# Scores on either kind of TensorE tiles, from exchanged copies of K and Q, in a windowed attention kernel

## The chip, the cores and the metric

The kernel runs on one core of one Trainium2 chip. The metric is device time in microseconds of one execution; of each kernel several runs are made and the median is taken. One profiled execution of the kernel before gives the views of the profile that are shown here.

Engines are named as the profile names them: PE (TensorE matmuls), PEld (its weight loads), DVE (VectorE), ACT (ScalarE), POOL (GpSimd) and SP (SyncE, which issues most of the DMAs; SPq is its queue).

## The reference

The input x is 224 × 224 pixels of 96 channels in bfloat16. One projection makes q, k and v. The first 48 channels attend within horizontal strips of 8 rows, the other 48 within vertical strips of 8 columns. A strip has 1,792 tokens and there are 28 of each kind. The two results stand side by side and go through a last projection.

```python
qkv = jnp.einsum('bhwc,cd->bhwd', x, wqkv)
...
scale = C2 ** (-0.5)
...
ah = _softmax(jnp.einsum('bqc,bkc->bqk', qh, kh) * scale, axis=-1)
oh = jnp.einsum('bqk,bkc->bqc', ah, vh).reshape(B, H, W, C2)
...
av = _softmax(jnp.einsum('bqc,bkc->bqk', qv, kv) * scale, axis=-1)
ov = jnp.einsum('bqk,bkc->bqc', av, vv).reshape(B, nw, H, sw, C2)
...
return jnp.einsum('bhwc,cd->bhwd', o, wo)
```

## The kernel before

**Blocks and halves.** Two strips make a block; there are 28 blocks (`P`), 14 horizontal and then 14 vertical. One strip lives on partitions 0 to 63 and the other on 64 to 127, of Q (`QT_sb`), K (`KT_sb`) and the values (`V_sb`). Every PE step of the main loop is a pair of matmuls, one for each strip (`w` is 0 or 1).

**Two kinds of tiles.** PE is used as four 64 × 64 tiles. A matmul whose operands lie on one half of the partitions can write to the same half or to the other half. When both strips write to their own half, the pair is on the *straight* tiles (mode "q"); when both write to the other half, it is on the *crossed* tiles (mode "v"). A step on straight tiles and a step on crossed tiles can run at the same time. Each kind has its own semaphore. Scores (`qk`, line 778) are on straight tiles and value products (`pv`, line 804) on crossed ones, except for the first four half key tiles (`turned`, `TURN = 2`), where it is the other way about. K, Q and most V projections (lines 535 and 637) are on straight tiles.

**A unit.** The queries of a block are cut in four chunks (512, 512, 512 and 256 columns). A unit is one chunk against 128 keys (256 for the short chunk): two score steps, called halves here, an exponential, and the products with V. There are 49 units in a block. Of 1,372 units 984 are ACT's: two halves fill two PSUM banks, one activation (line 824) reads both and writes one of eight `PT` buffers, two steps multiply by V. The other 388 are DVE's, taken in 194 pairs: DVE turns each half's scores into integers (line 844) in an `I_sb` buffer, two further operations (line 849, on POOL, or on DVE where the order says so) make `U_sb` and `E_sb` from it, and all three, read as bfloat16, are multiplied by V (`V_sb` twice, the scaled `Vs_sb` once). So a DVE unit has six value steps where an ACT unit has two. There are four buffers each of `I_sb` and `U_sb` (`NY`) and two of `E_sb` (`NL`). The first write of a pair into its `I_sb` waits for the products that read the pair `NY` back.

**The rest of a block.** `prep` projects K, Q and V of the next block from `xa_sb`/`xb_sb`, while the present one runs; DVE evicts them (lines 549, 556, 642). A chunk's sum is evicted to `OT_sb` (line 870) and projected by `wo` (lines 691, 725). Vertical blocks add the horizontal part from `Ph_sb` on POOL (line 733) and are stored by SP in 24 DMAs each (line 760). `blocks` (line 411) copies the input strips of a block into DRAM in block form, and `load` (line 418) transposes them into SBUF; both are on SP's queue.

**The order.** All operations are put in streams, one letter each. The string `SEQ` gives the order in which they are taken, and so the order on every engine; `BANK` gives the PSUM bank of each step that starts one. `Work.run` follows the strings and derives every wait from the operations' dependences, so an engine runs its list in order and waits where it must. The letters that the text uses: `a` a score half of an ACT unit, `A` its exponential, `c` its value step; `b` a score half of a DVE unit, `j` DVE's integer conversion, `U` or `u` the operations of line 849 on POOL or DVE, `d` and `D` the value steps with `I_sb`/`U_sb` and with `E_sb`; `e` evictions, `f` the projections, `h` the first of them; `X` and `x` loads and block transfers, `y` stores. `SEQ` and `BANK` were made ahead of time by a planner that isn't part of the kernel; the occupancies and latencies in the `Op` calls are its inputs and have no effect on the chip.

Of the kernel before, what the change touches and what calls it, by code (L numbers as in the profile page):

```python
# [23 lines left out]
def ndc(P, c):  # L24
# [9 lines left out]
    "fDjDAbcaceadfdAjdadaddecUdbAdadjafcDcAXXDebacajcbcUAcajcacbccAjcfaadodffAdbkeUadaddgjADbDacarjcbcAacrackcUjbdA"
    "fcacaejdfdAdabeadfdfUAXjcfabacecdAXcdadjabDdDAjbcacaDjfDAcaceUacDccAbaoaDcjbAgadardUjfdfAdfadradDfeADacaeccbVc"
    "fAajcaccbecAacjacUdbdAajdadbdjbddADaDajDdUDAacDcacbcDcAjdbacacjdUbAcajdadbdAodaDaDdjcdAcUdadagcbcArDcracacDcjA"
    "bcUacajgccAraodardbdgAdajUdadfDrAgarDacecfAcacreacUcbAdardadfdjdAbDaDeaDfDAdjacacdecdUAbdadjaDbDcAXXajcacbccAj"
    "bkcaUcacjcccAfadoadfdfAadaedkdbUcgAjcbDaDajcfcAacraecrbcfUcAjdadadebdAadadjdbdcdAXcjaUbaDdjDDAXabaffjDfAcDeacU"
    "accDAbcacjacccbcAoadaUdfjdAagadedffdfAracracDfDAebaUacecfcAcaedajdbdAadjbdadVdcjdAcbDaDjaDbDAdcUjacacbcdAcjaca"
    "cbcDAcjacUabDoAadadjdgddAdcrabraUcdDjdADbaDajDcbcAacjacfcUcAcaecagccAoadrardggUADaraDrddfrAdbrdacacjbcAUacacef"  # L40
    "cDAjDaDaDbecfAcaceacDdjbkdAadkajdDbdAjaUabdddddAXXjcacacbcAcjbacaUcccjcAfadaodfDfAbDaedadUgdjAdbacacrjcbcAaDra"
    "DDfjUDbAadadejdfdAadeaddcdcAXUbacajbdcdAXcDjabaDcjAcbUacacjcfcfAacaccfcbAoaaUcegAdadrajdfdAdraDaDfefdfAUabaecf"
    "ccjAbcacaecfcAcaVjcacbdedAadjbdadjbdAdUDaDajDdDbAcacjacbcdAcjaUcabdcDjbADcadajdAbdaodaUcdcdjcAdadagcbDrADDraca"
    "UcDcjbAcacajccgcAoaadrdbrUdgAdadrajDfDAdragacecfUAcacreaccfdAraddadbedfAdacajcbDADeaDajbkdDdkAcjdaUdaDbDcAXXaj"
    "cacbccAjbcacaUcjcccAfadoadfdfAadaedbdUDfAjDbcacaejcbcAacajcgdbUdArdajdadfrdAaDeaDdbdDAXUDjdabaccjdcAXfafafcbec"
    "DAacUacjcbcDAcajbacccjcAbadUaodfDAdjadadfdfefAaDageUcbcAracraccfjcAacacebcVcfAjadaddbedAadjbdaUDdDjdADbDacjacb"
    "cAdcjacaUcdbDAcajcabDoAdadadjUgdAdDarDarcdcbAcdajbadcDUcAjgaaccrDcrbAacacjccAUaodadbggAjdadadrdbArDaDarcjfUcAc"
    "acradfdedAadacebcfdAdjacacdDeAUbdaDajDbdADdjaDabcDjAXXcbcUacajcfcAcaecacbccAjafakcUofAdfdaaeddbAgdajdaDbDkrcAr"
    "aUcadjfdbdAcaecjadfcAcaceaUcfdfAXfadeabdDDdAXjafaDdbedADacaUjcDcbAcacjacbcDAcjabacccjcUAbaadodfDffAjadaddfedAa"
    "ceacVDbcfAjcacacbecAacUjadbddjbdAagadjdddDAaDrUaDrDbcdAjcaacbccdAcjabaUcDjcDAbacajdbddAjadacUcbocdAdaadjDgDdAc"  # L50
    "argarcDUcDArcarcacbcAccjcadaodbUAaDjaDcfcdgAbedadacrcjbAUdadadrfddAjgaadeddcAdcUarcarbdcAdDjabaDDjAfDaDaeUfcDc"
    "AXXaceacbccAjbacaccjkcccAfkadoaUdffAdaedadgdbArDfarDaccUejbAcacacjbcfdAdjadadbedAacacjbfdfAXcfjabUacDedDAXdadj"
    "abDdDAjDcacUacbcAcDjacaccccAbaoadUdfdjAdfadaedfDfAaDeagcfUcrAbracacedfAdadaeddjbAcVacajcbccAjbacaccjbDUAddaacj"
    "dcDbADaDjacbcdAcjdUcabaoDADajbadgddAjadUaDdrDdrcAbadajdcbcADcjacUagDcArcbrcacaccjAcaadoUdfdAadeadDgbDArdajcacf"
    "UcrAcbdaedadfdAjdadagebDADaDrajbDAcracUacdjcdAbdadjabcDcAXXDjcacaUcbcAacjacfcccecAfaodadbkdfUAgdjadadfrbDAraDa"
    "ceccAakjacUbddfjdbAdacaecjfdAdaceaUcdDdAXbaDajbdDdDAXDjabaDcUjcbAcacajccffAcfcaeacccUAcboaaddfjDAagaDedffAdfUr"
    "dardacfcAeabacecfdAcaVjcacbceAadjbdaddjbAddacacjUdDDAaDbaDcjbcdAacjacbcdcUAjabacDcjDbAadaodcAcjbUadadgjcdADdad"
    "rabrDdcADcjaUgacDrcAbrcacaccjcAaoadUdbdfAjdadadeDgbADacracjUbccAracagjcfdAdardeadfUdAcracaddecdAbacajDdbdDAjaf"
    "aDeDDDAXXbcaucaccAjbcakcakcjcccAfaodaUdfdfADbaeDaddgjAdbDaDarjUDbDAacracfcjcbAcacaejcfcAbadeaUdDdDAXdjabadddjd"
    "cAXdadabucfAcfacjacfcAbecacacjccAcbaoadUdfcAjaDaDbedfAfadjadfUdbAecaaccfjcAcbeacagcjVAdadadbrdfrdAadaDeUdDjdDA"  # L60
    "bcacjaDcbAcdjacacbUccdAjabaccDjDbAadaodDUAdjbadaDdcjdAcgadarbcrdcADUcacjacbcADcjagaccrcAoaUdardbdgAjdadadbrcfA"
    "rDDajcaUgcAaecacfcrDrAbcacadefdAdajdabdedAdUDaDajDdbAdadjabcDcDAXXjcaUcacbcfAcjacacccecAfaodakdbUDfADfjadadebd"
    "AdgaacrcrckcAUajadfdddbeAacajcbdfdAjcacaDdeDUdAXbdDajbaDDcAXDjabadcjcbUAcacjacffAcfcaeacccAbcUoadadfjdAbadaedf"
    "fAdfjaDgaDecbAUacrjaddbdAracacfcjcAacacVefdcbAecadajdbcdUAcjdcacaDbDAaDjbDacdcjdAbUacajcDbDAaodaddjbgAdaUDarDj"
    "dcdAcdardabcDcAjDgacUacrcbrAacacjccbAcoadajUdbAgdajgaddrdAbrDaDarcjfUcAcacracfcAedadadfedAdUadeabdcdcAjdbaDaDj"
# [12 lines left out]
    "DjbgAdadardfrdfAfdajdaDfDeAcaUcaecbcfAcjacacbecAacjacbcVcjbdAaaddjbddAdddaUjaDDbDdADjaabcDcjDAacabUcdcjbAcadaj"
    "dbddAoaDaDUdcjgcAdadrabrcdcADcjacacUbcADgjacaccrcAoaraddgbdUArdardadfDjADagaecfcAcUarceacbccAracadfjddAfdeadUa"
    "ddDeAdDabaDdjbdDAaDjaDkbcUcAXXjacacbccAjbcacacjcccAkfaUdoadfdfAdbaedadDgjADfacaUcercbrcfAcacjaccbAadeaddfqjfdf"  # L80
    "AabeaDfDUDAXjabaDdeddAXdcDjabaDcUjdAcacacbcdcAjfcacacfcbAUoaacjbfAdadaedgdjAdgVadacrcbrADaDarcjfcqcAarcaccfedb"
    "ADqaDajDbDAcjacUadbedAdjbacacdjbddAacacjUdccdAabacjbdcDADjadaUdboADaDadjbddcAdajdabcdcugAcacarcuDcDAcacraUcccj"
    "AgadardodbArdadadjgqDfAcracraDfcqecAacacedfdqAbddeaaccfUydjAbdacaeycDjAdbyaDaDjdbyADdkuadaDycDjcbAkacUyacjcbcA"
    "yacjaccfyocAbdayUjdadbAdfyajdadDfygDAfeacacyUcrcebArcyacadjfdyAdadeaDybDqfADfjaybaDjcfycAaUabedfydcAjdayadcdeb"
    "cAydcUajcacybcADcjacyacDbcoAyaUajbcygAdajdaXDgDrAdfradadUfrdfArcbacadeXdfAdjadacfcqebcAacaedddjXdcAqbDaDjaDbDA"
# [100 lines left out]
class Work:  # L186
# [29 lines left out]
    def run(s, seq, digits):  # L216
        at = {k: 0 for k in s.streams}
        digits = iter(digits)
        freed = {b: [] for b in range(8)}
        vlock = None  # L220
        for c in seq:
            both, q = c == "p", {"p": "P", "u": "U"}.get(c, c)
            op = s.streams[q][at[q]]
# [12 lines left out]
            if q != c:  # L236
                op.eng, op.fn = "dve", op.alt
# [697 lines left out]
```

## Time and profile before

| | us |
|---|---|
| median of 3 runs | 948.07 (947.41 to 948.56) |
| the profiled execution | 947.77 |
| its span, first to last instruction | 945.7 |
| busy: PE, ACT, DVE, POOL | 936.0, 925.2, 881.6, 769.2 |

The granted TensorE clock was 0.997 over the span. In a group of instructions the columns are line, engine, operation, output and inputs with their shapes, and the count; behind the bar the busy time in us, the mean duration of one in ns, and the idle time before them with what ended it. In a line of waits the numbers are total us, times, and the longest. In a line of the timeline they are start and duration in us. Records of one engine overlap, as an instruction starts while the one before drains, so a busy share close to 100% doesn't by itself say that an engine couldn't do more.

### The profile page before, as it was taken

To read this page: it belongs to the slowest core of one execution; us is meant where nothing else is said; L and a number is where in the kernel's file an instruction comes from. 1 tells how busy PE (TensorE), PEld (TensorE's weight loads), DVE (VectorE), ACT (ScalarE), POOL (GpSimd) and SP (SyncE) were. 2 spreads that over 40 slices of the span, in tenths; PEclk is the share of its full clock that TensorE was granted. 3 is DMA by queue.
4 is the path that set the end of the run, shared out by engine and by line. 5 is a ranking of instruction groups with operands and counts; after the bars stand their busy time and mean duration, and the time that the engine had idled before them with its cause. 6 is when DMAs were issued, how large, how long until landed. Compare 5 with 4: busy or idle time off the path is not lost.

```text
span 945.7 us, 48281 instructions
## 1 busy us (share of the span) xinstructions
PE 936.0 (99%) x21770; PEld 625.8 (66%) x21770; DVE 881.6 (93%) x1754; ACT 925.2 (98%) x993; POOL 769.2 (81%) x512
## 2 busy tenths in 40 slices
PE   9999999999999999999999999999999999999997
PEld 4666766676776677666666767766666666667664
DVE  8999999999999999999999999999999999999994
ACT  7999999999999999999999999999999999999996
POOL 3778988888886888787898888889879888878883
PEclk9999999999999999999999999999999999999998
DMA  8724513440441343244120515545533534461112
GB/s 141 96 46 72 71 22 53 71 66 9 71 71 22 52 72 47 28 71 71 28 46 10 93 36 81 88 72 86 86 61 67 85 57 81 76 84 30 31 20 44
DMA packets 253254, 57.09 MB, mean 60 GB/s; under 512 B 252936, under 2 KB 252936, under 8 KB 253048
## 3 DMA queue, kind: packets, MB, share of 16 engines
q1 hardware_dynamic: 251464, 53.47, 36.5%
q8 instruction: 170, 2.79, 1.3%
q10 hardware_dynamic: 1584, 0.55, 0.3%
q14 instruction: 36, 0.29, 0.1%
HBM read 19.13 MB, written 28.21 MB: 50 GB/s over the span
## 4 chain that ended last, share of the span: by engine, by line
PE 98%; ACT 1%; DVE 0%; issue 0%
PE ps L804 50%; PE ps L778 36%; PE ps L535 5%; PE ps L637 4%; PE ps L691 1%; PE ps L725 1%; ACT PT L824 1%; PE ps L396 0%; PE ps L602 0%; DVE out_sb L736 0%; PE ps L634 0%; PE ps L496 0%; PE ps L529 0%; DVE OT_sb L870 0%; DVE warm L368 0%
## 5 line engine op out<-in xcount | busy, mean ns | idle before, releaser
L824 ACT ACTIVATE PT<-ps 128x1024 bf16<-128x1024 f32 x984 | 921.2, 1036 | 7.7 <-PE ps L778 3.0
L778 PE MATMUL ps<-QT_sb,KT_sb 49*64 49x512 bf16 (+1 forms) x6272 | 738.8, 354 | 0.7 <-issue 0.6
L844 DVE TENSOR_SCALAR I_sb<-ps 128x512 int16<-128x512 f32 x776 | 511.1, 682 | 21.7 <-PE ps L778 17.2
L804 PE MATMUL ps<-PT,V_sb 64*50 64x512 bf16 (+1 forms) x4496 | 499.4, 350 | 0.2 <-issue 0.2
L778 PEld LDWEIGHTS ps<-QT_sb,KT_sb 49*64 49x64 bf16 x6272 | 282.3, 105 | 159.0 <-ACT PT L824 53.7
L849 POOL TENSOR_SCALAR U_sb<-I_sb 128x2048 int16<-128x2048 int16 x170 | 322.5, 1897 | 55.6 <-DVE I_sb L844 37.0
L849 POOL TENSOR_SCALAR E_sb<-I_sb 128x2048 int16<-128x2048 int16 x164 | 311.1, 1897 | 46.2 <-PE ps L804 18.9
L804 PE MATMUL ps<-U_sb,V_sb 64*50 64x512 bf16 (+1 forms) x1776 | 245.7, 350 | 0.0
L804 PE MATMUL ps<-I_sb,V_sb 64*50 64x512 bf16 (+1 forms) x1776 | 239.7, 352 | 0.2
L804 PEld LDWEIGHTS ps<-PT,V_sb 64*50 64x50 bf16 x4496 | 215.6, 100 | 32.7 <-issue 0.7
L804 PE MATMUL ps<-E_sb,Vs_sb 64*50 64x512 bf16 (+1 forms) x1776 | 233.2, 350 | 0.0
L733 POOL TENSOR_TENSOR out_sb<-tmp,Ph_sb 128x480 bf16<-128x480 f32 (+1 forms) x84 | 85.7, 1028 | 31.0 <-DVE E_sb L849 14.9
L804 PEld LDWEIGHTS ps<-I_sb,V_sb 64*50 64x50 bf16 x1776 | 80.2, 100 | 31.4 <-PE ps L804 8.2
L804 PEld LDWEIGHTS ps<-U_sb,V_sb 64*50 64x50 bf16 x1776 | 89.2, 100 | 14.0
L804 PEld LDWEIGHTS ps<-E_sb,Vs_sb 64*50 64x50 bf16 x1776 | 88.0, 100 | 13.8 <-issue 0.6
L535 PE MATMUL ps<-xa_sb,w_sb 64*64 64x512 bf16 (+3 forms) x440 | 80.2, 356 | 0.2 <-issue 0.2
L870 DVE CAST OT_sb<-ps 128x512 bf16<-128x512 f32 x112 | 68.9, 615 | 9.2 <-PE ps L804 8.5
L535 PE MATMUL ps<-xb_sb,w_sb 64*64 64x512 bf16 (+2 forms) x436 | 77.1, 348 | 0.0
L556 DVE TENSOR_SCALAR_CACHE_REDUCE KT_sb<-ps,bias 128x512 bf16<-128x512 f32 x108 | 72.0, 677 | 1.9 <-PE ps L535 1.5
L549 DVE TENSOR_SCALAR QT_sb<-ps 128x512 bf16<-128x512 f32 (+1 forms) x111 | 67.5, 615 | 3.2 <-PE ps L535 1.8
L637 PE MATMUL ps<-w_sb,xa_sb 64*64 64x48 bf16 x1512 | 65.3, 187 | 0.0
L637 PE MATMUL ps<-w_sb,xb_sb 64*64 64x48 bf16 x1512 | 64.9, 186 | 0.1
(68 smaller groups left out, 604.0 us busy)
## 6 DMA issues: line engine op xcount, KB each, us to landing
x_blocks<-in_x_dram SPq DMA_DIRECT2D x54, 336.0 KB
out_dram<-out_sb SPq DMA_DIRECT2D x104, 42.0 KB
out_dram<-out_sb SPq DMA_DIRECT2D x208, 21.0 KB
out_dram<-out_sb SPq DMA_DIRECT2D x22, 24.0 KB
xa_sb<-x_blocks SPq DMA_TRANSPOSE x27, 5.0
xb_sb<-x_blocks SPq DMA_TRANSPOSE x27, 5.9
Ph_sb<-in_x_dram ACTq DMA_DIRECT2D x1, 336.0 KB, 3.1
out_dram<-out_sb ACTq DMA_DIRECT2D x6, 24.0 KB
```

The costliest lines, as they stand in the source:

```text
L535: ins = e.matmul(out_, lhsT=wt, rhs=rhs, start=i == 0, stop=startup or i == 1)
L549: return e.tensor_scalar(dst, src, QS if startup else A128, None, ALU.mult)
L556: return e.tensor_scalar(dst, src, bias[:, 0:1], None, ALU.add, ALU.add, accum_out=acc)
L637: ins = e.matmul(out_, lhsT=(xa_sb, xb_sb)[i][b][o:o + 64, 0, t0:t0 + 64], rhs=w2_sb[o:o + 64, i, wblk(P, "v"), 0:C2], start=i == 0, stop= ...
L691: ins = e.matmul(bk3[to:to + 64, s, :], lhsT=OT_sb[b][o:o + CA, blk * 64:(blk + 1) * 64], rhs=wo_sb[0][o:o + CA, :], start=True, stop=True)
L733: return e.tensor_tensor(res, tmp[t][:, 0:n, :], ph, ALU.add)
L778: ins = e.matmul(bank(t.k)[to:to + 64, i * qs:(i + 1) * qs], lhsT=KT_sb[b][64 * w:64 * w + CA, 64 * k:64 * k + 64], rhs=QT_sb[b][64 * w:64 ...
L804: ins = e.matmul(bank(k_.slot.k)[to:to + CP, 0:qs], lhsT=V_[o:o + 64, k, :], rhs=rhs()[o:o + 64, h * 512 + i * qs:h * 512 + (i + 1) * qs], ...
L824: a = wk.add("A", Op("act", ACT, lambda e: e.activation(split(PT[i % NPT]), two(ts), ACTF.Exp, scale=LN128), qs_ + pt_free.get(i - NPT, [] ...
L844: ds.append(wk.add("j", Op("dve", 0.6, lambda e, t=t, at=at: e.tensor_scalar(I_sb[y][:, at:at + 512], bank(t.k), one, 0.0, ALU.add, ALU.ma ...
L849: fn = lambda e, dst=dst, c=c: e.tensor_scalar(dst[:, 0:m], I_sb[y][:, 0:m], float(c), 1.0, ALU.add, ALU.mult)
L870: k.evac = wk.add("o", Op("dve", 0.07 + qs / 960, lambda e, k=k, b=P % 2, q0=q0, qs=qs: e.tensor_copy(OT_sb[b][:, q0:q0 + qs], bank(k.slot ...
```

## The change

There are second copies of Q and K, `QS_sb` and `KS_sb`, with the two halves of the partitions exchanged. They are made by four DMAs within SBUF for each block, on SP's queue (stream `w`; for block 0 stream `x`): two for K and two for Q. A score half can be computed from them too. Its operands then come from the other half of the partitions, so the same result in the same place is made by the other kind of tiles. The order says which: letters `n` and `m` are `a` and `b` from the copies.

To make room, `NY` goes from 4 to 3. The evictions into K and Q, and the copies, wait for the last scores of either kind of two blocks ago; the K and Q projections themselves no longer do. `turn_w` moves to stream `h`, and the block transfer of block 2 moves behind block 0's copies. `SEQ` and `BANK` are new throughout. The number of exponentials, of DVE units and of all PE steps stays the same; operations of line 849 on DVE go from 54 to 51.

```diff
@@ Work.run
-        vlock = None
+        vlock, last = None, {}
         for c in seq:
-            both, q = c == "p", {"p": "P", "u": "U"}.get(c, c)
+            both, q = c == "p", {"p": "P", "u": "U", "n": "a", "m": "b"}.get(c, c)
             op = s.streams[q][at[q]]
             at[q] += 1
             deps = list(op.deps)
+            if c in "nm":
+                dep, op.mode, op.fn = op.other
+                deps.append(dep)
+            if op.pair is not None:
+                last.setdefault(op.pair, {})[op.mode] = op
+            if op.war is not None:
+                deps += last.get(op.war, {}).values()
...
-            if q != c:
+            if c in "pu":
                 op.eng, op.fn = "dve", op.alt
@@ buffers
-    NPT, NY, NL, NR, NT = 8, 4, 2, 4, 3
+    NPT, NY, NL, NR, NT = 8, 3, 2, 4, 3
...
+        QS_sb = [sb(f"QS_sb{i}", [128, NTOK], BF16) for i in range(2)]
+        KS_sb = [sb(f"KS_sb{i}", [128, NTOK], BF16) for i in range(2)]
...
+        s_alt = [sem(f"s_alt{b}") for b in range(2)]
@@ blocks: a planner's input
-                ops.append(wk.add(stream, Op("sp", 1.4, lambda e, dst=dst, src=src: e.dma_start(dst, src), [], lat=7.0, dma=s_xs[P % 4])))
+                ops.append(wk.add(stream, Op("sp", 1.4 if is_h[P] else 2.6, lambda e, dst=dst, src=src: e.dma_start(dst, src), [], lat=7.0, dma=s_xs[P % 4])))
...
         load(1, "x")
-        blocks(2, "x")
...
@@ prep
-            qk_war = list(last_qk[prev2].values()) if prev2 >= 0 else []
+            qk_war = list(last_qk[prev2].values()) + [alt_ready[prev2]] if prev2 >= 0 else []
...
-                              pe_fn, xs + [op_w0] + (mean_ev.get(P, []) if kind == "q" else []) + qk_war, evs, mode="p" if startup else "q", steps=1 if startup else 2)
+                              pe_fn, xs + [op_w0] + (mean_ev.get(P, []) if kind == "q" else []), evs, mode="p" if startup else "q", steps=1 if startup else 2)
                 xt_read[P][p.stream] = p
+                ops[0].war = prev2
...
+            war = list(last_qk.get(prev2, {}).values())
+            for dst, src, ready in ((KS_sb[b], KT_sb[b], k_ready[P]), (QS_sb[b], QT_sb[b], q_ready[(P, NCH - 1)])):
+                for w in range(2):
+                    alt_ready[P] = wk.add("w" if P else "x", Op("sp", 0.64, lambda e, dst=dst, src=src, w=w: e.dma_start(dst[64 - 64 * w:128 - 64 * w, :], src[64 * w:64 * w + 64, :]),
+                                                  [ready] + war, lat=3.0, dma=s_alt[b]))
+                    alt_ready[P].war = prev2
@@ qk
-                def fn(e, t=t, th=th):
-                    for i, k in enumerate(th):
-                        for w in range(2):
-                            to = 64 - 64 * w if turn else 64 * w
-                            ins = e.matmul(bank(t.k)[to:to + 64, i * qs:(i + 1) * qs], lhsT=KT_sb[b][64 * w:64 * w + CA, 64 * k:64 * k + 64],
-                                           rhs=QT_sb[b][64 * w:64 * w + CA, q0:q0 + qs], start=True, stop=True)
-                    return ins
-                ops.append(wk.add(stream, Op("pe", S, fn, [k_early[P] if kts[-1] < 2 else k_ready[P], q_ready[(P, c)]], steps=len(kts), take=[t], book=ts[1:] if pair and not h else [], mode="v" if turn else "q")))
-            last_qk[P][stream, turn] = ops[1]
+                def score(alt, t=t, th=th):
+                    K_, Q_ = (KS_sb[b], QS_sb[b]) if alt else (KT_sb[b], QT_sb[b])
+
+                    def fn(e):
+                        for i, k in enumerate(th):
+                            for w in range(2):
+                                to = 64 - 64 * w if turn else 64 * w
+                                o = 64 - 64 * w if alt else 64 * w
+                                ins = e.matmul(bank(t.k)[to:to + 64, i * qs:(i + 1) * qs], lhsT=K_[o:o + CA, 64 * k:64 * k + 64],
+                                               rhs=Q_[o:o + CA, q0:q0 + qs], start=True, stop=True)
+                        return ins
+                    return fn
+                o = wk.add(stream, Op("pe", S, score(False), [k_early[P] if kts[-1] < 2 else k_ready[P], q_ready[(P, c)]], steps=len(kts), take=[t],
+                                      book=ts[1:] if pair and not h else [], mode="v" if turn else "q"))
+                o.other, o.pair = (alt_ready[P], "q" if turn else "v", score(True)), P
+                ops.append(o)
+            last_qk[P][stream] = ops[-1]
@@ main
         prep(0, startup=True)
+        blocks(2, "x")
```

More of the change, by code (lines that the diff above doesn't have):

```diff
@@ L34 @@
[L34 to L53, printed above, removed]
@@ new lines @@
+    "cAjnadDfdUAdfnaddeAdbaaceDfcjbccAaadcegbjdAckwaXadwrAdcbajdkdrajAddcUbacacjbUXdDAjdDnnDbDDjDAcfnaccUffAfcacaec"
+    "cAcccaeamfoddAndjafddXfefcAUanedfDaDXfbAaefcfdbAjaacecAcfjaaegcdfAdeDaaddrcUVDAbwddraacwdjAbDDacjabcAdjccacUac"
+    "bdcAcbjnacDjcADanodbUDAcjfddnnddedADcmandUjcmcAcDjancgcAdcrDrgnacccUrAcnradboddAajaDbdcfdjDAaacceUbAcfjdanddbe"
+    "AdaadjdUAgbdcarcjacgrcAbanjDcdddAcXrXracadDcUcmADaDjamccDAcjDnafcccAcfeanodfwdfAbdewadaDdcUgjbkAadkajcbDAcaacr"
+    "jUcdrcAbfdaaejddbdAdXfjaDUabDcdeAXDaajcDdffAfanemUcdAcDjcancmcdAjcbacajccDUAcbnnjccbcAoaDafddddAUaaDddfdeffAca"
@@ new lines @@
+    "acjefUAccadabfddceAajaVbcceAcjacbwadcddDjdAaawgDUcbcdAarajDDDAcrdcbcnUajDcbAccaodaDdfAdjdnnceDgcdAaraccdrmdcAj"
+    "caabcAdcbjUDanDgcjcArcnaorAmjdgdaaUdrdbAcdadDjacbrcDAfnjUacADbegaaddrbjdddaAardcdUAjddaabcdXjfADDeDaacfUccAanm"
+    "ecwDjccmAacajcbDcAccjckaaXcUmkcfoAanwdjdffdAbeadadUdjgDAbrcjaaccbcADaarcfcUjcbDAXeDaajcAaDfXaddfeUAffmdeadadcd"
+    "dAdjcaaDAmccjdanbdUccjcDbAcanjcccAoDcabnfdUdfAddeaaddDffbjAaaecAdDfUdjaacebdfAcdeaaccdddjwdAbVcaagwjdAccrdacac"
+    "rbcUADDajbnDDjADbccaacjbccUDAjacacodmdfAnaddddecacAUnjgcDdacaAbrrjDDADgUacacrdrbccAaajcccAcmoanfdjbddAedUacajg"
@@ new lines @@
+    "dcbADaaDrjfDDADdarXabUDecfAdaaecjdddbwjnAdwngddAcrcdaabDcdcrcAaUacjmkkAcdcacjacXbDcAcbcajncUcjcfAanodUdffdbAed"
+    "aadDdgjbAcraaDcjccAbcraaUjfccbAXedaajcddfAXeamdndddDUAdjDaamDDcAfcfjancfdUcAecaabcccADDjmancjdccAcbanodfUdDaAd"
+    "eadfcjdffAaabecADjfcaacbedccfAdadaUedjdbwAgVajaDdrdwdcddArDaaccDdAcbUaaDcbDjUAccaacjbcAcDjccaacbodfAdanjdddddc"
+    "aAeUcbacjAdDgDarcacrbDDAcanjUcbccccjaAgadrdobddAraaddjDgbADaracjccUcbAraacbddjcAfdjaacdUbecAaadDgfdcjrAandrcdU"
+    "edAcXDXaaccmADjdmDanccDDjfAUcaeccamwcAocfanddfwjfAdbkDaeaddgdkjAbDaraccjUcAcbcraacfDbjcAaacDejbDfUADXjanddfeAX"
@@ new lines @@
+    "dffnaedddmAfUanecdcddcAjanmcdDcjcAabnUcDcjccAbcjancboddAaadUfdffAdaeafcdjAcbaadcjbVADcaacejfddDbAdUaacedjdaAda"
+    "wgrcdwdrbADDjcUacadDbAcDajcacbcDcAjcaabcDUccAbjaaDddofdAandedddUADcjbaacDdcjcAangcrcDAcUrbacacccjcAgadroadrdAb"
+    "gdDraadjDbdAaracccfUjAnaegcfADrDecaaUdccbDrAajabddfAcdjddbdnDndeccADjnkaXdbdjcAmXcnaccjcwAbccUjaaDkwfccAconnUf"
+    "dfAdeDbaajfdDbAddaenUjbdgAcccaabrAjccdrnafjDbdUAcXaendjAXdcfffancmeAdddjcdaaAmDdDDcnjacDacdAnbUcUcbjcDAaacjccc"
+    "AcbnoadUfddAddfaadefDbfAajaDcecfAcjcaaccebAfddaaeddbjAwgaUcjardwAddcdcdranDbDdaDjAabcDcAcUDcjaabDccbcaAjcaVdjc"
@@ new lines @@
+    "dmAdoUnndUcdddAcjcabadDcjbAcaacDjbUcAjDcangDcrcccgArandroddAbUdaraDfjddAneafcAbDeUdacafccdcjAaeadcbcgdAdajadgr"
+    "rbrAcnDnDjdDdDAXXranUcmcjcdDmAancjcAdbcjDcanUbccAjcccaUnfdddbodAaeadgDbjwdAaradcdjbcaArdabjDXcdaAawfUjdmdkcfAf"
+    "anjDcddecdAmXkanccUjbcADDdjaacfcDADeDnabcUcfcAjaaccccceAcUnadodfdffAneadfaddAebfaccfcfbAjaaDedDAUjfacacceAbfdd"
+    "aedagdjdDAdwaVarDwrdADbDacajcAbccjcDaUabcdcAjcbccaajcDcdAanobfdUDAjDdgnnddrcdAdceabracUdccjAdbaaccbjDcDAjcancc"
+    "UcmAoanfdjdAddfeaneDUAcbdaafcdbjDAceacacjwbAgDDajabrcdArDgadradjDdmdAdrnnwdjcAXUXcdUdgnarcdDmrccakAUajccbccADa"
@@ new lines @@
+    "cjabcccAjcfandfodfAbkdUedaaDAjcgDraacdrcAbfcaUcaeDjcbfdDAjanDbdeAXddfaacDjdfAXdfnUncdddebAaUacjcmdAcdjcanccbcc"
+    "AjDanbccDjcAcbanodUdfAdaaecdfDdffdAjaacfDecabAeagcdcArajacrcAcbfUedaadjdcVwbdAanDddbjdwAcUaDacbdjAcDaacDjUdcbA"
+    "cjacaDccDboAandfjddDAeandmUddAdjDnnmDcdcjcgAanrDcUrcbcAcaacjbcccAcjgaadrdobUAdrdaaDddgjbArDcjaacfAdcUacrafceAc"
+    "caegaDbdddArajadbrdcdAaDndjbdADdXbaXjUaDDcjAccbacacjcfAecDacabUwcccAcfjwanokDcfdfADaadgebUAcdaardrdbdjAccaabjc"
+    "aAcckajdUdbjAfXddadaedmDdAXdcjaaDUDfAedDaacmcDcAcjdanDbUccccAjaamcccjcfAandofdfUAdadeadfgDAaaeDcbcrAracacjfcdf"
@@ new lines @@
+    "fAUabeaDjdAfDaDaccebAdfaeVdadDjwdAddbajcawccdAbUaccajcbUcDcAajbnDccdAjdcnaoAdabDajfdgDAcaUadrddcderbAaaDcjbcAa"
+    "jUacgDdccArcrabndccccAmjanddoAdjfdeaadgdUAbcaaccrjADcbraaDbccfjcXAUdadjaeAdfddecXnnbDcjdAakaddgDrdkrDAbdUawnDj"
+    "ccDDAmjacwaccbUAcjcacabcccfAjanDodffAUfdadabedADdejnabdccgAfjnUacrcdecAXbaradddfcfAXjfanddebDcdAdajaccfDAUaacD"
+    "DDDebUAcaadbjccdAjaaccbccAccjcanfdfdofAaeadbdddfaAVjacebAcccfaacjbDUAeDjagawdbdcAjddawadrrUccbddAaacjdcbAcDjaa"
+    "dccAdDbuDaajDccAbUcDjcaacDbAoanfdDjdDgAaeUdaDAdcrDcdarbacdjcdAbacjacbcUcAdjagacccrcArmaadDdodfjdAaadeUgdbADcar"
@@ L165 @@
+    "40237654072364576237456321546321754632174562376547234675032467032406742310674132076412307643201467132417632547"
+    "61325167452314675321576123576123506752317605231760132576032506752304675234765432761523415672431567234156723476"
+    "54320675423057643205674023567452346753241673241765324167523167432761403216741234671325467132546713246512375641"
+    "234532165402361054326501432561052360165321075632176032561276325154"
 )
 class Op:
-    __slots__ = ("eng", "occ", "lat", "fn", "deps", "take", "give", "wait", "dma", "own", "mode", "lock", "alt", "book", "stream", "steps", "sync")
+    __slots__ = ("eng", "occ", "lat", "fn", "deps", "take", "give", "wait", "dma", "own", "mode", "lock", "alt", "book", "stream", "steps", "sync", "other", "pair", "war")
@@ L174, in __init__ @@
         s.steps = steps
-        s.sync = []
+        s.sync, s.other, s.pair, s.war = [], None, None, None
         s.dma, s.own, s.mode, s.lock, s.alt, s.book, s.wait = dma, own, mode, lock or eng == "pool", alt, list(book), None
@@ L456, in bass_standalone__window_attn_cswin__vision_kernel @@
                 chunks[(P, c)] = k
+        alt_ready = {}
         ksum_op, mean_pe, mean_ev, q_pe, wqT_op = {}, {}, {}, {}, []
@@ L643, in vv @@
                 xs = [x_op[P], op_w2] if not startup else [x_tr] + x_cols(64 * k0, 64 * (k0 + n))
-                cut = [0, n] if startup else [0, 4, 7, n] if k0 == 0 else [n * i // 3 for i in range(4)]
+                cut = [0, n] if startup else [0, 2 * TURN, n] if k0 == 0 and TURN > 2 else [0, 4, 7, n] if k0 == 0 else [n * i // 3 for i in range(4)]
                 part = list(zip(cut[:-1], cut[1:]))
```

213 lines of the change are left out of this document (98 added, 115 removed).

## The prediction

> **What bounds the kernel now.** I read the page's busy line first, then its chain and its costliest groups.
>
> ```profile
> span 945.7 us, 48281 instructions
> ...
> PE 936.0 (99%) x21770; PEld 625.8 (66%) x21770; DVE 881.6 (93%) x1754; ACT 925.2 (98%) x993; POOL 769.2 (81%) x512
> ...
> PE 98%; ACT 1%; DVE 0%; issue 0%
> ...
> L824 ACT ACTIVATE PT<-ps 128x1024 bf16<-128x1024 f32 x984 | 921.2, 1036 | 7.7 <-PE ps L778 3.0
> L778 PE MATMUL ps<-QT_sb,KT_sb 49*64 49x512 bf16 (+1 forms) x6272 | 738.8, 354 | 0.7 <-issue 0.6
> L844 DVE TENSOR_SCALAR I_sb<-ps 128x512 int16<-128x512 f32 x776 | 511.1, 682 | 21.7 <-PE ps L778 17.2
> ```
>
> Three engines are above 90%, and the two that look full are not: records of one engine overlap. ACT's own limit has to be read from starts. The first answer below is line 824's (its count, then minimum, median and maximum, then first and last start); the second is ACT in order of time near the end, where almost nothing else is left to run.
>
> ```profile
> L824 ACT ACTIVATE PT<-ps x984: 1018/1024/1168, 9.7 to 936.5; 128x1024 bf16<-128x1024 f32 x197
> ```
>
> ```profile
> 927.51 10.19 ACT L824 ACTIVATE PT<-ps 128x1024 bf16<-128x1024 f32 x11
> ```
>
> Over the whole program 983 strides take 936.5 − 9.7 = 926.8 us, 0.943 us each. Near the end ten strides take 936.5 − 927.5 = 9.0 us, 0.90 each. At that pace 983 strides would take 885 us. So 42 us are lost between exponentials, though the wait column shows only 7.7: a wait shorter than the overlap of two records doesn't show as idle time. This 42 us is all that ACT can win. The rest of the span is 9.7 us of start and 9.2 us behind the last start.
>
> What ACT lacks in those gaps is scores, by the waits:
>
> ```profile
> PEld ps L778 <- ACT PT L824: 53.7, 218, 0.5
> ...
> DVE I_sb L844 <- PE ps L778: 17.2, 60, 1.0
> ...
> ACT PT L824 <- PE ps L778: 3.0, 9, 0.9
> ```
>
> The first is the loop itself: a score matmul waits for the exponential two units back to free its two banks, and once they are free, both halves run one behind the other on one kind of tiles. Anything already queued on that kind (a VectorE unit's score, a K, Q or V fill) comes first and pushes the exponential back.
>
> DVE sets the second limit. The windows by half of the steady run (PE, PEld, DVE, ACT, POOL busy):
>
> ```profile
> 60.00:470.00 410.00, 409.26 (x9704) 276.75 (x9698) 382.79 (x754) 406.80 (x436) 340.76 (x206) 1.00 0.33 51
> 470.00:900.00 430.00, 429.90 (x10164) 290.00 (x10162) 414.98 (x821) 427.26 (x457) 365.92 (x255) 1.00 0.41 65
> ```
>
> In the horizontal part DVE has 27 us free of 410, in the vertical part 15 of 430. ACT could gain 410 − 436 × 0.90 = 18 us in the first; DVE allows at most 15 in the second. With some 3 us from the start phase (to 60 us), 36 is the ceiling.
>
> **The change part by part.** *Scores on either kind.* The new order has 492 flipped halves (letters n 356, m 136) of 2,744. From each half's own kind by its key tile, 307 move to the crossed tiles and 185 to the straight ones. 276 of the 984 exponentials now have one half on each kind, where before every one had both on the same. What a split is worth shows in this stretch of PE:
>
> ```profile
> 121.51 0.38 PE L804 MATMUL ps<-U_sb,V_sb 64*50 64x512 bf16 x2
> 121.73 0.38 PE L778 MATMUL ps<-QT_sb,KT_sb 49*64 49x512 bf16 x2
> 121.83 0.40 PE L804 MATMUL ps<-I_sb,V_sb 64*50 64x512 bf16 x2
> 121.95 0.38 PE L778 MATMUL ps<-QT_sb,KT_sb 49*64 49x512 bf16 x2
> 122.07 0.38 PE L804 MATMUL ps<-I_sb,V_sb 64*50 64x512 bf16 x2
> 122.16 0.38 PE L778 MATMUL ps<-QT_sb,KT_sb 49*64 49x512 bf16 x2
> 122.28 0.59 PE L804 MATMUL ps<-U_sb,V_sb 64*50 64x512 bf16 x6
> ```
>
> On one kind matmuls follow at 0.22 us (121.73, 121.95). A split pair is ready one such step sooner if both kinds are free, and gains nothing if the other kind is as far behind: between 0 and 276 × 0.22 = 61 us, cut to 36 by the ceiling. I take the share: 28% of the pairs are split, and 28% of the 42 us is 12 us. It is below the middle because flips can't help where DVE is the limit.
>
> *Load of the two kinds.* A net 122 halves go to the crossed tiles, 122 × 0.22 = 27 us. By the order's counts at 0.22 us a step, crossed tiles had some 860 us of work against 848 and get 886 against 821. Before, crossed tiles were thus idle for some 86 us of the span; at 939 us, 53 are left. That covers it, so I cost it at nothing, and at 27 us if those gaps can't be filled. What speaks for filling them: the order now lets the value products (c) run a median of 5 exponentials behind theirs instead of 4, so more work is waiting.
>
> *Order within PE.* Neighbours of the same kind rise from 1,308 to 3,022 (mostly "aa" and "cc" where "ac" alternated). In the stretch above the program's letters are d a a b d, all crossed, then d d, straight: the straight I_sb product starts at 121.83, ahead of a (121.95), b (122.16) and d, which stand before it. So the other kind passes up to three waiting steps, and a run of two or three costs nothing. A rule speaks against this: the Trainium skill's page "TensorE: Matmul & The Clock Gate" (Part 3, The mechanism) has matmuls strictly in program order, with only weight loads pulled ahead. By it the new runs would hold back the other kind; the trace disagrees, by these rows.
>
> *Copies.* Each block gets four copies on SP, two of K, two of Q: 112 copies of 64 rows of 3,584 B, 224 KB. No copy within SBUF of that size is in the trace; nearest are:
>
> ```profile
> xb_sb<-x_blocks SPq DMA_TRANSPOSE x27, 5.9
> Ph_sb<-in_x_dram ACTq DMA_DIRECT2D x1, 336.0 KB, 3.1
> ```
>
> The plain load in long rows (3.1 us) is nearest in kind; 5.9 us is the far end. In the order the first flipped score of a block stands 4 to 9 exponentials, median 5, behind the block's last copy: 5 × 0.94 = 4.7 us. At 3.1 us nothing waits. Issue costs SP 112 × some 0.6 us = 67 us of an engine that mostly waits. Queued behind a waiting copy on SP are stores, block transfers and the next loads; those loads stand some twenty exponentials ahead of their use. A block transfer fills the DMA engines:
>
> ```profile
> 471.00:477.00 6.00, 1.00 0.93 138
> ```
>
> In the last third one half of a block transfer often stands just ahead of the Q copies, a few us in the worst blocks. I take 1 us in all.
>
> *Three I_sb/U_sb buffers instead of four.* This adds a wait: the first I_sb write of a pair of DVE units waits for the products that read the pair three back. Behind it on DVE stand the K and Q evictions and all other I_sb writes, and PE and ACT wait for their banks. Before, a median of 35 PE steps lay between that last product and the write in the order; now 7, at the 5% point 3.5. Two kinds work at once, so 7 steps are 7 × 0.11 = 0.8 us. A value product can still be three steps (0.66 us) behind its place plus 0.38 us of its own record, so some pairs will wait. Nothing to 0.3 us for half of the 194 pairs, 0 to 29 us; I take 2 us, as DVE's free 15 and 27 us absorb the usual short one.
>
> *Small edits.* Three E/U operations go from DVE to POOL:
>
> ```profile
> L849 POOL TENSOR_SCALAR U_sb<-I_sb 128x2048 int16<-128x2048 int16 x170 | 322.5, 1897 | 55.6 <-DVE I_sb L844 37.0
> ...
> L849 DVE TENSOR_SCALAR U_sb<-I_sb 128x2048 int16<-128x2048 int16 x24 | 17.1, 714 | 0.0
> ```
>
> 3 × 0.71 = 2.1 us less on DVE, 5.7 more on POOL, which is 81% busy: nothing, and part of the share above. The weight turn moves ahead in the start; block 2's transfer moves behind block 0's copies, with over twenty exponentials before its block is needed; K and Q fills no longer wait for old scores, only their evictions do. Each nothing, ±1 us.
>
> *Sum.* −12 + 0 + 1 + 2 = −9 us. The profiled execution took 947.77 us, 0.3 below the median of 948.07. So 938.8, say 939 us.
>
> **The rivals.** *The shorter ring costs DVE (slower).* Place: the first I_sb write of each pair. Half of 194 pairs at 0.3 us is 29 us; DVE has no other cover in the vertical part, and the gain shrinks with it: 947.8 − 12 + 1 + 29 − 10 absorbed in the horizontal part = 956 us. It decides above some 0.1 us per pair (12 us over 97). For it: the margin of 7 steps. Against, the same wait before:
>
> ```profile
> DVE I_sb L844 <- PE ps L804: 0.2, 1, 0.2
> ```
>
> *The copies land late (slower).* At 5.9 us plus 0.6 of issue against 4.7, the first flipped score stalls PE 1.8 us in 27 blocks, with all that is behind it; about 0.9 is covered by the exponential at work: 27 × 0.9 = 24 us, 947.8 − 12 + 24 + 2 = 962 us. It decides from a landing of some 5 us. Against: no transposition is in these copies.
>
> *The change does nothing.* Crossed tiles become the bound and the split pairs find them behind: 948 ± 1 us.
>
> *More than the share.* Splits sit where the straight tiles are behind: 24 us, two thirds of the ceiling, less 3: 927 us.
>
> *Strict order.* If a waiting step held back the other kind and every second extra neighbour cost a step, 857 × 0.22 = 189 us, 1,137 us. The rows above leave it little chance. This is what the page's rule named there would make of the order.
>
> **How the numbers follow.** The share 0.45 (932 to 946); more 0.15; nothing 0.08; ring 0.20; copies 0.10; strict order 0.02. A change under 0.2% (1.9 us) is about what a measurement of this kernel can't tell from none. Faster 0.45 + 0.15 = 0.60, same 0.08, slower 0.32. Range 926 to 958: it takes in the larger gain and the ring's 956, and leaves out the late copies, strict order and the outer parts of the others. The likeliest case alone: 932 to 946.
>
> **What would show it.** Right: line 824's stride from first to last start falls from 0.943 to about 0.933; DVE over 97% busy in the vertical part; the wait of line 778 on ACT no larger. Wrong by the ring: DVE's I_sb writes wait on line 804. Wrong by the copies: weight loads of line 778 wait on a DMA of KS_sb or QS_sb. Wrong by the load: line 824 waits on line 778 though neither shows.

## The result and the profile after

The changed kernel takes 959.89 us (median of 4 runs, 958.64 to 961.26) against 948.18 us before (the runs named above and one more): a ratio of 1.0123, 95% interval 1.0111 to 1.0135. It is 11.7 us slower. The prediction was 939 us, with a range of 926 to 958: the change went the other way.

The lines of the page that answer to those of before (lines moved: 824 is now 851, 778 is 801, 804 is 831, 844 is 871):

```profile
span 956.8 us, 48444 instructions
...
PE 939.8 (98%) x21770; PEld 646.4 (68%) x21770; DVE 882.2 (92%) x1751; ACT 924.9 (97%) x993; POOL 776.0 (81%) x515
...
PE 90%; DMA 4%; DVE 2%; ACT 1%; issue 1%; SPq 1%
PE ps L831 44%; PE ps L801 33%; PE ps L650 5%; PE ps L547 4%; DMA QS_sb<-QT_sb 4%; ACT PT L851 1%; PE ps L710 1%; PE ps L744 1%; DVE I_sb L871 1%; DVE QT_sb L561 1%; SPq L679 0%; PE ps L408 0%; DVE V_sb L655 0%; PE ps L615 0%; DVE out_sb L755 0%
...
L801 PE MATMUL ps<-QS_sb,KS_sb 49*64 49x512 bf16 (+1 forms) x1148 | 173.8, 351 | 7.0 <-DMA QS_sb<-QT_sb 6.8
...
KS_sb<-KT_sb SPq DMA_DIRECT2D x56, 224.0 KB, 3.4
QS_sb<-QT_sb SPq DMA_DIRECT2D x56, 224.0 KB, 3.5
```

The busy times of ACT and DVE are those of before; only the gaps grew. The chain has a member that it did not have: the copy of Q, with 4% of the span. The profiled execution took 958.64 us.

The exponentials of the kernel after (count, then durations, then first and last start), and the two halves of the steady run:

```profile
L851 ACT ACTIVATE PT<-ps x984: 1018/1024/1179, 9.6 to 946.0; 128x1024 bf16<-128x1024 f32 x197
```

```profile
60.00:470.00 410.00, 407.22 (x9596) 280.66 (x9590) 378.18 (x740) 402.20 (x431) 345.54 (x210) 1.00 0.46 80
470.00:900.00 430.00, 425.38 (x10034) 295.78 (x10030) 410.36 (x812) 421.81 (x451) 359.96 (x251) 1.00 0.53 93
```

The mean stride rose from 0.943 to (946.0 − 9.6) / 983 = 0.953 us. In the horizontal part 431 exponentials start where 436 did, in the vertical part 451 where 457 did. PE, which had no gap of note, is idle for 2.8 and 4.6 us. The waits say on what:

```profile
PEld ps L801 <- ACT PT L851: 39.9, 165, 0.6
...
ACT PT L851 <- PE ps L801: 9.8, 21, 1.8
...
PE ps L801 <- DMA QS_sb<-QT_sb: 6.8, 9, 1.8
PEld ps L801 <- DMA QS_sb<-QT_sb: 6.6, 7, 2.1
...
DVE I_sb L871 <- PE ps L831: 3.4, 10, 0.6
```

PE stands still for copies for 6.8 us, in nine places; a block has one such place at most, at its first flipped half. The row of the weight loads shows mostly the same stalls a second time, so the two rows can't be added. The wait of DVE for the shorter ring is 3.4 us. One place in order of time, SP first, then the weight loads, then ACT:

```profile
74.21 1.13 SPq L679 DMA_DIRECT2D QS_sb<-QT_sb  x2
75.45 2.25 SPq L430 DMA_TRANSPOSE xa_sb<-x_blocks  x1
```

```profile
78.52 0.43 PEld L831 LDWEIGHTS ps<-U_sb,V_sb 64*50 64x50 bf16 x8
79.73 0.11 PEld L801 LDWEIGHTS ps<-QS_sb,KS_sb 49*64 49x64 bf16 x2 [0.78 <-DMA QS_sb<-QT_sb]
```

```profile
75.76 3.82 ACT L851 ACTIVATE PT<-ps 128x1024 bf16<-128x1024 f32 x4
80.40 1.94 ACT L851 ACTIVATE PT<-ps 128x1024 bf16<-128x1024 f32 x2 [0.81 <-PE ps L801]
```

The two Q copies of block 2 are issued from 74.21 on. The first flipped half goes on at 79.73, 5.5 us later, and with it everything behind it in PE's order. The weight loads had been idle since 78.95, 4.7 us behind the first issue. ACT has by then run out: 0.81 us of visible idle time.

### The profile page after: what moved, and what is told of

It reads as the page before. It is cut to its first block, busy times and chain, and to the rows that moved or that the text cites. A ratio compares the mean times of both kernels' runs of the same rounds, so it can differ in the third digit from the quotient of the medians.

```text
span 956.8 us, 48444 instructions
## 1 busy us (share of the span) xinstructions
PE 939.8 (98%) x21770; PEld 646.4 (68%) x21770; DVE 882.2 (92%) x1751; ACT 924.9 (97%) x993; POOL 776.0 (81%) x515
## 4 chain that ended last, share of the span: by engine, by line
PE 90%; DMA 4%; DVE 2%; ACT 1%; issue 1%; SPq 1%
PE ps L831 44%; PE ps L801 33%; PE ps L650 5%; PE ps L547 4%; DMA QS_sb<-QT_sb 4%; ACT PT L851 1%; PE ps L710 1%; PE ps L744 1%; DVE I_sb L871 1%; DVE QT_sb L561 1%; SPq L679 0%; PE ps L408 0%; DVE V_sb L655 0%; PE ps L615 0%; DVE out_sb L755 0%
## 5 line engine op out<-in xcount | busy, mean ns | idle before, releaser
L801 PE MATMUL ps<-QT_sb,KT_sb 49*64 49x512 bf16 (+1 forms) x5124 | 650.3, 355 | 0.4 <-DVE KT_sb L568 0.2
L831 PE MATMUL ps<-PT,V_sb 64*50 64x512 bf16 (+1 forms) x4496 | 537.1, 350 | 0.1
L876 POOL TENSOR_SCALAR E_sb<-I_sb 128x2048 int16<-128x2048 int16 x169 | 321.1, 1900 | 41.5 <-PE ps L831 15.5
L801 PEld LDWEIGHTS ps<-QT_sb,KT_sb 49*64 49x64 bf16 x5124 | 237.1, 105 | 120.4 <-ACT PT L851 33.3
L831 PE MATMUL ps<-E_sb,Vs_sb 64*50 64x512 bf16 (+1 forms) x1776 | 264.2, 350 | 0.0
L831 PE MATMUL ps<-U_sb,V_sb 64*50 64x512 bf16 (+1 forms) x1776 | 264.0, 350 | 0.0
L831 PE MATMUL ps<-I_sb,V_sb 64*50 64x512 bf16 (+1 forms) x1776 | 254.3, 351 | 0.1
L801 PE MATMUL ps<-QS_sb,KS_sb 49*64 49x512 bf16 (+1 forms) x1148 | 173.8, 351 | 7.0 <-DMA QS_sb<-QT_sb 6.8
L831 PEld LDWEIGHTS ps<-I_sb,V_sb 64*50 64x50 bf16 x1776 | 85.6, 100 | 24.4 <-PE ps L831 6.7
L801 PEld LDWEIGHTS ps<-QS_sb,KS_sb 49*64 49x64 bf16 x1148 | 58.9, 105 | 33.3 <-ACT PT L851 6.6
```

The source lines that it names most:

```text
L801: ins = e.matmul(bank(t.k)[to:to + 64, i * qs:(i + 1) * qs], lhsT=K_[o:o + CA, 64 * k:64 * k + 64], rhs=Q_[o:o + CA, q0:q0 + qs], start=Tr ...
L831: ins = e.matmul(bank(k_.slot.k)[to:to + CP, 0:qs], lhsT=V_[o:o + 64, k, :], rhs=rhs()[o:o + 64, h * 512 + i * qs:h * 512 + (i + 1) * qs], ...
L876: fn = lambda e, dst=dst, c=c: e.tensor_scalar(dst[:, 0:m], I_sb[y][:, 0:m], float(c), 1.0, ALU.add, ALU.mult)
```

## The experiments

Each ratio below is to the kernel before, run on the same chip. Not all runs had the same chip, and the kernel before took 947.3 to 948.7 us on them, so a difference of two medians from different chips is sure to about 1 us.

**All flips undone.** In the order, each `n` becomes `a` and each `m` becomes `b`; copies and ring stay.

```diff
-SEQ = ...
+SEQ = ... with "n" -> "a", "m" -> "b"   (492 letters)
```

> All 492 flipped halves back on their own kind; the order, the copies and the ring of three stay. Late copies: the 13.4 us of waits on QS_sb go and nothing else is lost, because outside the ten strides around each block's first flipped half the mean stride was 0.943, as before: about 950 us. Flips are worth their 12 us elsewhere: 13 us gained and 12 lost, 958 to 960 us. Ring: stays at 959 or above.

Measured 986.53 us, ratio 1.0403 (1.0388 to 1.0419). None of the three: the waits on copies went (the 13.4 us counts the stalls twice), and it is 27 us slower. So in this order the flips are worth a great deal, and the order without them is 38 us worse than the old one. The old order can't be seen as "the new order without the flips". What changed with the letters can be counted in the order. Runs of five or more steps on one kind of tiles: 10 before, 21 after, 116 here. The prediction's stretch of PE showed three waiting steps being passed by the other kind, one more in execution; a run of five or more goes beyond what it showed. The traces show the limit. If each matmul is given its place in the order, no step of the kernel before, the changed kernel or this one starts ahead of more than three earlier ones; ahead of three start 6, 19 and 91 steps. How much of the loss the long runs hold is worked out below, under the share of 28%; no run changes them alone.

**Near flips undone.** Only the flips that stand fewer than 8 exponentials behind their block's last Q copy go back.

```diff
-SEQ = ...
+SEQ = ... with 76 of the "n"/"m" -> "a"/"b"
```

> Only the 76 flipped halves that stand fewer than 8 exponentials behind their block's last Q copy go back to their own kind; 416 flips stay. Late copies: no matmul waits for a copy any more, about 950 us. Ring or load of the crossed tiles: 957 to 960 us, since both stay nearly as they were.

956.30 us, 1.0087 (1.0072 to 1.0102). The waits on copies are gone, and 3.6 us are won: between the two expectations. 76 flips fewer also cost something: at 0.033 us each (the least that the last run below gives) to 0.078 us (38.5 us against the kernel before, for 492), that is 2.5 to 6 us. Both together put the late copies at some 6 to 10 us, an estimate.

**Q copied by chunk.** The first 512 columns are copied as soon as they are evicted, on a semaphore of their own, the rest at the old place.

```diff
-            for dst, src, ready in ((KS_sb[b], KT_sb[b], k_ready[P]), (QS_sb[b], QT_sb[b], q_ready[(P, NCH - 1)])):
+            for dst, src, ready, c0, c1 in ((KS_sb[b], KT_sb[b], k_ready[P], 0, NTOK), (QS_sb[b], QT_sb[b], q_ready[(P, 0)], 0, 512), (QS_sb[b], QT_sb[b], q_ready[(P, NCH - 1)], 512, NTOK)):
...
-                o.other, o.pair = (alt_ready[P], "q" if turn else "v", score(True)), P
+                o.other, o.pair = ([alt_first[P]] + ([alt_ready[P]] if c else []), "q" if turn else "v", score(True)), P
```

> All flips stay. The copy of Q is made in two parts: columns 0 to 511 as soon as the first chunk is evicted, the rest where it was; flipped halves of the first chunk wait for the first part alone. Late copies: the waits on QS_sb fall below 2 us in total, about 950 us, as in the run with the near flips undone. Ring or load: 957 to 960 us.

964.64 us, 1.0158 (1.0131 to 1.0184): slower than both expectations, and telling by half. The windows (ACT alone; the last columns are the granted clock, the DMA share and GB/s):

```profile
60.00:470.00 410.00, 404.97 (x435) 1.00 0.47 80
470.00:900.00 430.00, 411.54 (x439) 0.99 0.52 90
```

In the horizontal part 435 exponentials start, against 436 before and 431 after: four of the five are back. In the vertical part it is far worse, by three long waits. They, and SP's queue ahead of the longest, which ends at 720.9:

```profile
PE ps L803 <- DMA QS_sb<-QT_sb: 10.6, 3, 6.1
```

```profile
712.18 0.72 SPq L424 DMA_DIRECT2D x_blocks<-in_x_dram  x1
712.94 4.08 SPq L781 DMA_DIRECT2D out_dram<-out_sb  x3
717.06 0.53 SPq L680 DMA_DIRECT2D QS_sb<-QT_sb  x1
717.63 0.63 SPq L781 DMA_DIRECT2D out_dram<-out_sb  x1
718.30 0.53 SPq L680 DMA_DIRECT2D QS_sb<-QT_sb  x1
```

The last Q copies stand behind stores, and three of these, issued just behind a block transfer, take 4.08 us where others take some 0.6 each. Ahead of the second longest wait a copy itself stands behind a block transfer: it takes 3.26 us to issue and lands 7.2 us after its start. With these two waits the granted clock went to 0.50 for 6.8 and 3.4 us, most of it behind the wait, so the time lost is more than the waits.

**Block transfers moved ahead.** On the chunk run, the vertical blocks' transfers go to just behind the K copies. Two runs more stood on the same base: one with 106 flips to the crossed tiles undone, one with all 185 flips to the straight tiles undone.

```diff
-SEQ = ... "X" (block transfers 16 to 27) where they were
+SEQ = ... "X" behind the second K copy of the block (transfer 26: behind the Q copies)
```

> As the copies by chunk, with the block transfers of the vertical part moved ahead of (one of them behind) the Q copies, so that no copy queues behind one. Late copies: the three jumps of the chunk run (2.6, 8.7 and 4.2 us) go, 949 to 952 us. If the copies were not the loss: 958 us or more.

988.94 us, 1.0430 (1.0412 to 1.0447). The expectation of 949 to 952 fell, because the move made the copies later:

```profile
566.44 5.81 SPq L680 DMA_DIRECT2D QS_sb<-QT_sb  x2
572.29 9.06 SPq L781 DMA_DIRECT2D out_dram<-out_sb  x14
581.40 0.53 SPq L680 DMA_DIRECT2D QS_sb<-QT_sb  x1
```

The first copies are stuck for 5.81 us behind the block transfers, this pushes 14 stores back, and the last Q copies stand behind those. The horizontal part, which the move left alone, kept its 435.

```diff
-SEQ = ... of that run
+SEQ = ... with 106 "n"/"m" -> "a"/"b" (first run) or 185 others (second run)
```

> The run before, with 106 flips to the crossed tiles undone where a run of one kind gets no longer than two by it: crossed 853 us of work, straight 835, nearly as in the old order. Load of the crossed tiles: at least 5 us below the run before, 943 to 947 us. Flips worth their average of 0.078 us each (38.5 us for 492): 8 us above it, 958 us.

> The same base with all 185 flips to the straight tiles undone: crossed 916 us of work, straight 772. Load of the crossed tiles: about 40 us more on the bound, 975 us or more. Average worth of a flip: 185 x 0.078 = 14 us above the base, 964 us.

989.53 us (1.0442, 1.0427 to 1.0458) and 997.91 us (1.0527, 1.0512 to 1.0543). As totals they say little, since the vertical part is spoilt in all three. In the horizontal part 435, 432 and 422 exponentials start (base, 106 undone, 185 undone). So lightening the crossed tiles does not help. Loading them costs more than an average flip, but with the 185 flips undone runs of five or more rise from 21 to 65 as well, so this is not the load's alone.

**Copies first.** On the chunk run, in the vertical part, the stores and block transfers that stood between a block's first and last Q copies go behind them.

```diff
-SEQ = ... w w y y y ... X w w        (Q copies of a vertical block)
+SEQ = ... w w ... w w X y y y
```

> Q copied by chunk again, and in the vertical part the copies really first on the queue: the stores and block transfers that stood between a block's first and last Q copies are issued behind them. Late copies as the whole loss: no jump of over 1.5 us is left in the vertical part, 948 to 951 us, the old kernel's time and not better. If flips are worth something once copies are in time: 940 to 946 us. If something else costs the 11 us: 957 us or more.

961.26 us, 1.0146 (1.0131 to 1.0161). Two long waits were left, on a load that the reordering itself had made late:

```profile
PEld ps L548 <- DMA xb_sb<-x_blocks: 8.9, 2, 5.0
```

In two blocks the next block's load now stood behind the stores. That led to the run after the next.

**Copies delayed on purpose.** The changed kernel, with two copies of no use ahead of each block's Q copies; the order gets 54 more `w` for them.

```diff
+                for i in range(2) if dst is QS_sb[b] and P else ():
+                    dums[i] = wk.add("w", Op("sp", 0.64, lambda e, src=src, i=i: e.dma_start(warm[64:128, 256 * i:256 * i + 256], src[0:64, 0:256]), [ready] + [d for d in [dums.get(i)] if d], lat=3.0, dma=s_dum[i]))
```

> The changed kernel with two small copies of no use (64 rows of 512 B into the tile of the start-up matmuls) on the queue ahead of each block's Q copies, some 1.2 us of issue in 27 blocks. Copies are what the first flipped half waits for: 27 x 0.6 to 27 x 1.2, 976 to 992 us. If copies land in time in most blocks: up to 5 us more, 960 to 965 us.

991.58 us, 1.0444 (1.0417 to 1.0471): 31.7 us above the changed kernel. PE waits for copies in 20 places instead of nine:

```profile
PE ps L805 <- DMA QS_sb<-QT_sb: 28.2, 20, 3.6
```

The 31.7 us are 27 times 1.17 us, as if all of the added issue time reached the end, but the halves differ:

```profile
60.00:470.00 410.00, 396.04 (x425) 1.00 0.45 79
470.00:900.00 430.00, 400.53 (x426) 0.98 0.53 93
```

By the starts of the exponentials the profiled execution loses 8.5 us over the 13 delayed blocks of the horizontal part, where their issue adds some 15 us, and 24.2 us over the 14 vertical ones, where it adds some 16. Nine of the 27 blocks lose under 0.3 us. In the vertical part five of the stalls come with stretches at a granted clock of 0.50, 20.4 us in all; the changed kernel has none before its end. So the first flipped half has less than 1.2 us of slack in most blocks, not none in all, and the match with 27 × 1.17 us is a coincidence.

**Copies and loads in time.** The run with the copies first, and in blocks 19 and 20 the stores go behind the load that they had been ahead of.

```diff
-SEQ = ... w w y y y X              (blocks 19 and 20)
+SEQ = ... w w X y y y
```

> The run with the copies first, with one thing mended: in blocks 19 and 20 the stores no longer stand ahead of the next block's loads. Late copies as the whole loss: the two jumps of 6.7 and 5.2 us, which fell on waits for xb_sb, go, 948 to 951 us. Something else: 955 us or more.

951.46 us, 1.0034 (1.0021 to 1.0047). 8.4 of the 11.7 us are back, with all flips, the ring of three and the new order kept. In the second view, of the flipped operands, no wait on a copy is left: its idle list begins with ACT and DVE.

```profile
60.00:470.00 410.00, 404.79 (x434) 1.00 0.45 79
470.00:900.00 430.00, 425.01 (x455) 1.00 0.54 94
```

```profile
its engine sat idle before it (us, times) until:
  ACT PT L853: 5.9, 23
  DVE I_sb L873: 2.5, 11
```

**The ring and the copies' traffic.** Two runs without flips and copies, with four and with three buffers.

```diff
-    NPT, NY, NL, NR, NT = 8, 3, 2, 4, 3
+    NPT, NY, NL, NR, NT = 8, 4, 2, 4, 3
```

> No flips, no copies, and the ring of I_sb and U_sb back to four; the order is the new one. Late copies alone: the same as with all flips undone, about 950 us. Ring: 3 to 10 us below the run with all flips undone. If the order itself is as good as the old one, 946 to 950 us.

> No flips and no copies, with the ring of three. Against the runs with all flips undone (with copies and three: 986.5; without copies and with four: 985.3) it splits 1.3 us between the copies' traffic and the ring: 985.3 if it is the traffic, 986.5 if it is the ring.

985.26 us (1.0389, 1.0374 to 1.0405) with four and 985.27 us (1.0395, 1.0379 to 1.0410) with three; 986.53 with the copies. The ring costs nothing in this order, though DVE waits 5.4 us for it with three buffers and 1.7 us with four, and the copies' traffic costs some 1 us (1.3 by the medians, 0.8 by the ratios of the two runs with three buffers). Both were measured in an order that is 38 us slower. In the changed kernel the row for the ring says 3.4 us of DVE's waits; no run has four buffers together with the copies, so what the ring costs there stays open.

**Load of the crossed tiles.** On the run with copies and loads in time, 106 flips to the crossed tiles are undone.

```diff
-SEQ = ...
+SEQ = ... with 106 of the "n"/"m" -> "a"/"b"
```

> The run with copies and loads in time (951.5 us), with 106 flips to the crossed tiles undone where a run of one kind gets no longer than two by it: crossed 853 us of work, straight 835. If the load of the crossed tiles is what eats the gain: 943 to 948 us. If it is not, each undone flip costs up to its average worth of 0.078 us: 952 to 960 us.

956.14 us, 1.0071 (1.0053 to 1.0089): 4.7 us slower than its base by the medians, 3.5 us by the ratios; 0.033 to 0.044 us for each undone flip. The two kinds are as evenly loaded as in the old kernel, and it doesn't help. Between first and last start the profiled execution takes 4.5 us more; the 98 exponentials whose pair of halves the undone flips changed lose 4.8 us, 0.049 each, and the other 885 together gain 0.2 us. There are no more long runs here than in the base (19 against 21), so this is the worth of the flips by themselves.

## Why the prediction was wrong

**Copies: the step that failed.** They were put at 1 us, from 3.1 us of landing against a distance of 4.7 us to the first flipped half. They cost 8.4 us (from 959.9 to 951.5 when they come in time, in a run that also moves stores and transfers on the queue). Two things were off. The price was of one transfer: the median over all 112 copies is 3.4 to 3.5 us, not far from 3.1, but the first flipped half needs the last of two issued in a row. This one lands a median of 4.1 us after its own issue, at most 6.5, and 3.9 to 7.9 us after the first one's. And the distance of 4.7 us was a median: in ten of the 27 blocks it is four exponentials, 3.8 us. So nothing was left over, and nine blocks waited. The delayed run shows it: 1.2 us more of issue let 20 blocks wait.

The rival of late copies named this mechanism and the point where it decides (a landing of some 5 us), with a chance of 0.10. Its 962 us was the nearest of all, but by two errors that cancel: its 24 us was too much, as PE stood still in nine blocks, 0.8 us each, where it had 27 at 1.8 us, and it too counted on 12 us of gain. The block transfers, "a few us in the worst blocks", were named, and behind them three copies of the changed kernel took 1.9 to 3.0 us to issue; the 1 us in all underpriced them too.

**The share of 28%: the second step that failed.** It took the 42 us of lost stride and gave the split pairs their part, 12 us. Once copies come in time, the stride is still no better than before:

```profile
L853 ACT ACTIVATE PT<-ps x984: 1018/1025/1178, 9.6 to 939.4; 128x1024 bf16<-128x1024 f32 x197
```

(939.4 − 9.6) / 983 = 0.946 us, against 0.943. The flips do work: undoing all costs 27 us, undoing 106 costs 3.5 to 4.7. What they earn, the new order has already spent, as it is 38 us behind the old one without them. The share compared flips with the old order, and there was no run in which they stood in it.

Where the order without flips loses can be read from the starts, as it takes the exponentials in the same order as the run with copies and loads in time. Between first and last start it is 35.8 us slower. The 276 exponentials with a split pair lose 20.2 us of this when the pair is made whole; the 114 right behind a run of five or more lose 15.3; 60 are both, and their 8.8 us are in both sums. Away from long runs a former split pair loses 0.053 us and any other 0.014. So a split is worth some 0.04 to 0.05 us in this order, about what the prediction gave it (12 / 276 = 0.043). By this the size was about right and the starting point wrong. Long runs are a part of the loss, not all of it; why the planner's order without flips is so much worse is otherwise open.

Of the 11.7 us, 3.3 stay when copies are in time; about 1 of that can be the traffic, the rest stays open.

**Load of the two kinds at nothing: right.** The rival that crossed tiles take the gain away fell in two comparisons (435 to 432 exponentials, and 3.5 to 4.7 us slower). Loading them further with 185 undone flips did cost, 13 exponentials in the horizontal part, but that order also has 65 long runs, so the load is not shown to be the cause.

**Order within PE: right within its limits.** Neighbours of one kind rose by 1,714 and no strict order showed: 957 us of span, not 1,137. The Trainium skill's page "TensorE: Matmul & The Clock Gate" (Part 3, The mechanism), which has matmuls in program order, does not agree with these traces, where 19 steps of the changed kernel start ahead of three earlier ones. But "a run of two or three costs nothing" does not go on for long runs: none starts ahead of four, and the exponentials right behind long runs lose most (0.13 us each).

**Ring: 2 us taken, small as forecast.** DVE waits 3.4 us for it in the changed kernel, against 0.2 before, and the pair of runs in the slower order shows no cost. The rival that had the highest chance of the slower ones, at 956 us, came near the time by the wrong mechanism.

**DVE and small edits:** three operations moved to POOL; DVE's busy time stayed within 0.6 us (881.6 to 882.2), nothing as predicted.

## What to carry to other kernels

When work is made to depend on a new transfer, price the last of its parts from the first issue to landing, with what is ahead on its queue, and look for the slack of its first reader, not for the median distance. A cheap test of that slack is to delay the transfer on purpose and to see, block by block, how much of the delay reaches the end. The total alone can mislead, as stalls here came with stretches of half clock. When an order is remade for a new freedom, the freedom's worth can't be read off the old order's losses: the remade order may lean on it and be worse without.

## What the runs showed that was not expected

Issuing a copy on SP behind a block transfer takes up to 5.81 us for two instead of 1.13, so in these rows a transfer of many short rows holds back the issuing engine as well as the data, and stores behind it move too.

A stall of PE can cost twice. In the delayed run five stalls of 1.8 to 3.6 us came with 3.4 or 6.8 us at a granted clock of 0.50, for the most part behind the stall, and in the chunk run two of 2.6 and 6.1 us with 3.4 and 6.8 us. Others of up to 2.2 us did not.

And PE's freedom to let one kind of tiles pass the other is large but bounded: no step started ahead of more than three earlier ones. 492 flips back in place, with 116 runs of five or more steps on one kind in place of 21, cost 27 us though no step was added.
